# Windowed attention and mixture of experts: the product of P and V with 16 matmuls of 130 columns, and attention's pipeline one step longer

## The chip, the core and the metric

The kernel runs on one core of a Trainium2 chip. The core has five engines with queues of their own: TensorE (PE, its weight loads are shown as PEld), VectorE (DVE), ScalarE (ACT), GpSimd (POOL) and SyncE (SP), which here issues nearly all DMAs. The metric is the device time of one execution in microseconds (us).

## What is computed

Attention over 8 batches, 8 heads, 576 positions of 64 values. The first four heads see the last 32 positions, the other four see every fourth of the last 128. Its output, one row of 512 values for each of 4608 tokens, goes through a two-level choice of one expert out of 16 and that expert's two layers (512 to 1024 to 512).

```python
scores = scale * np.matmul(q, k.transpose(0, 1, 3, 2))
mask_plain = (rel >= 0) & (rel < window)                                   # heads 0 to 3
mask_dil = (rel >= 0) & (rel < window * dilation) & (rel % dilation == 0)  # heads 4 to 7
scores = scores - np.max(scores, axis=-1, keepdims=True)
attn = np.exp(scores)
attn = attn / (np.sum(attn, axis=-1, keepdims=True) + 1e-09)
out = np.matmul(attn, v)
...
for g in range(G):            # group by argmax of x @ w_group, expert by argmax of xg @ w_expert
    h = np.maximum(xg[mask_e] @ w1[g, e], 0.0)
    out[tok_idx] = combined[:, None] * (h @ w2[g, e])
```

## The kernel before

Attention runs as 36 tiles (`NT`), nine (`NJ`) for each of four pairs of batches. The dilated heads are laid out so that they are windows of 32 as well. A tile n holds 64 query positions of two batches and eight heads, in two halves a of 32 queries, and each half sees 64 keys. The main loop runs over steps s, and in one step several tiles are in work, each in another stage:

- `scores(s)`: a matmul with the identity puts the mask into PSUM (L263), then 16 float32 matmuls of 128 rows by 32 columns of weights (the queries) and 128 columns of keys are added (L275). DVE takes the row maxima (L285) and subtracts them (L286).
- `softexp(s)`: ACT takes the exponentials and writes p (L291).
- `transpose_p(s-1)`: PE turns p with four 128x128 transposes (L298), ACT copies the result to one of two buffers pt (L299).
- `av(s-2)`: 32 float32 matmuls (L308), each with 64 rows by 32 columns of weights (a piece of P turned) and 65 columns of V, which are 64 values and a column of constants that gives the softmax denominator. Half a = 1 reads V as loaded (`vt`), half a = 0 reads a copy shifted by 32 positions (`vs`), which POOL makes in `shift_v(s+2)` (L125, L131). ACT copies the denominators (L318).
- `normalise(s-2)`: DVE takes reciprocals (L334) and multiplies (L336) to x; `store(s-2)`: SP writes x to DRAM with two DMAs (L349).
- `transpose_x(s-3)`: four transposes (L360), which ACT copies to xT (L362, L364).

In between, `spend` runs pieces of the routing of a pair of batches whose nine tiles are complete (`route`, up to a budget of 1.8 in the units of a table of costs for each step): matmuls L377, L388, L447, L449, L524, and many small DVE operations. From the middle on, `run(wq)` loads one chunk of expert weights in a step (L630) and splits it into two float16 parts on ACT and DVE (L644, L641). At the last steps `run(eb[0], ...)` adds early pieces of the experts' layers. After the loop the experts follow one after the other: L759 (first layer), L818 (second), L740 (turning gathered rows).

The queues of PE, ACT, DVE and SP run in the order in which this code is written (`manual_schedule`); POOL's order is set by the tile framework's scheduler. In a step SP issues, in this order, the loads of q(s+4), k and v(s+3) and the two stores of x. Each waits for its buffer to be free, and each DMA on SP signals one of eight semaphores in turn, so that an issue also waits until the DMA eight issues earlier has landed.

A float32 matmul appears in the trace as two weight loads and two matmuls, a transpose or a 16-bit matmul as one of each.

Of the kernel before, what the change touches and what calls it, by code (L numbers as in the profile page):

```python
# [8 lines left out]
F32 = mybir.dt.float32  # L9
# [3 lines left out]
AF = mybir.ActivationFunctionType  # L13
ALU = mybir.AluOpType
# [3 lines left out]
P = 128  # L18
B, H, S, D = 8, 8, 576, 64
# [5 lines left out]
NJ = S // 64  # L25
NT = NBP * NJ
# [4 lines left out]
SCALE = 0.125  # L31
# [14 lines left out]
NWST2 = 3  # L46
BUDGET = 1.8
COST = (0.21, 0.3, 0.21, 0.62, 0.36)
NQ, NK, NV, NVS, NPT = 4, 6, 5, 4, 2
EARLY_STEPS = {NT - 1: 1, NT: 2, NT + 1: 2, NT + 2: 2}  # L50
TAIL = (
    "R0w0wr0rrrrrrrrrrr1rrrr0rr1r1rr1r1rr1rrB1w12w1ww112w2w2w2w2O2O2O2O2O2O"
# [12 lines left out]
def moe_attention_kernel(ctx, tc, q, k, v, cmask, wgate, wpack, out):  # L65
    nc = tc.nc
# [11 lines left out]
    id32 = cp.tile([P, P], F32, name="id32")  # L78
# [16 lines left out]
    att = ExitStack()  # L95
    apool = lambda name, bufs=1, **kw: att.enter_context(tc.tile_pool(name=name, bufs=bufs, **kw))
    psA = apool("psA", 1, space=PSUM)
    vp = apool("vp", NV)
    qp = apool("qp", NQ)
    kr = apool("kp").tile([P, 2, 2 * NK, 8, 32], F32, name="kr")  # L100
    pt = [apool(f"pt{i}").tile([P, 4, P], F32, name=f"pt{i}") for i in range(NPT)]
# [15 lines left out]

    def load_v(n):
        if n < NT:
            vt[n] = vp.tile([P, 8, 65], F32, name="vt")  # L120
            nc.sync.dma_start(vt[n], v[n])

    def shift_v(n):
        vs[n] = vp.tile([P, 8, 65], F32, name="vs", bufs=NVS)
        nc.gpsimd.tensor_scalar(vs[n], vt[n], 1.0, 1.0, ALU.mult, ALU.mult)  # L125
        for r in range(2):
            odd = slice(64 * r, 64 * r + 32)
            if n % NJ == 0:
                nc.gpsimd.memset(vs[n][odd], 0.0)
            else:  # L130
                nc.gpsimd.tensor_scalar(vs[n][odd], vt[n - 1][odd], 1.0, 1.0, ALU.mult, ALU.mult)  # L131

    nc.vector.memset(kr[:, :, 0 : NK + 1 : NK], 0.0)
    nc.sync.dma_start(masks[:, 0:2], cm[:, 0:2])
# [82 lines left out]
    ap = apool("ap", 3)  # L217
# [69 lines left out]
        dd[n] = d  # L287

    def softexp(n):
        p = ap.tile([P, 8, 64], F32, name="p", bufs=2)  # L290
        nc.scalar.activation(p, dd.pop(n), AF.Exp, scale=SCALE)  # L291
        st[n] = p

    def transpose_p(n):
        p = st.pop(n)
        t = psT.tile([P, 4, P], F32, name="t", tag="t")
        for c in range(4):
            nc.tensor.transpose(t[:, c, :], p[:, 2 * c : 2 * c + 2, :].rearrange("p a b -> p (a b)"), id32)  # L298
        nc.scalar.copy(pt[n % NPT], t)  # L299

    def av(n):
        o = psA.tile([P, 2, 512], F32, name="o", tag="o")
        for c in range(4):
            for w in range(2):
                for bb in range(2):
                    for a in range(2):
                        j = bb * 2 + a
                        nc.tensor.matmul(  # L308
                            o[32 * j : 32 * j + 32, w, c * 65 : c * 65 + 65],
                            pt[n % NPT][64 * w : 64 * w + 64, c, 32 * j : 32 * j + 32],  # L310
                            (vs, vt)[a][n][64 * w : 64 * w + 64, bb * 4 + c, :],
                            start=True,
                            stop=True,
                        )
        oo[n] = o
        den = ap.tile([P, 2, 4], F32, name="den")
        ov = o[:, :, 0:260].rearrange("p k (s c) -> p k s c", c=65)
        nc.scalar.activation(den, ov[:, :, :, 64], AF.Copy, bias=1e-9 / SX)  # L318
        dn[n] = den
# [10 lines left out]
    def normalise(n):  # L330
        o = oo.pop(n)
        ov = o[:, :, 0:260].rearrange("p k (s c) -> p k s c", c=65)
        den = dn.pop(n)
        nc.vector.reciprocal(den, den)  # L334
        x = ap.tile([P, 4, 2, 64], F32, name="x", bufs=5)
        nc.vector.tensor_tensor(  # L336
            x.rearrange("p s w c -> p w s c"),
            ov[:, :, :, 0:64],
            den.unsqueeze(3).broadcast_to([P, 2, 4, 64]),
            ALU.mult,  # L340
        )
        st[n] = x

    def store(n):
        x = st[n]
        bp, J = n // NJ, n % NJ
        for bb in range(2):
            row = (2 * bp + bb) * S + 64 * J
            nc.sync.dma_start(xd[row : row + 64], x[64 * bb : 64 * bb + 64].rearrange("p s w c -> p (s w c)"))  # L349
# [546 lines left out]
    man = ExitStack()  # L896
    ET = mybir.EngineType
    man.enter_context(tc.manual_schedule(engines={ET.PE, ET.Activation, ET.DVE, ET.SP}))
    for s in range(NT + 3):
        ripe = bool(gate)  # L900
        if s < NT:
            scores(s)
        if 0 <= s - 1 < NT:
            transpose_p(s - 1)
        if 0 <= s - 2 < NT:
            av(s - 2)
        if s < NT:
            softexp(s)
        if 0 <= s - 2 < NT:
            if ripe:  # L910
                gate.clear()
            normalise(s - 2)
        if start:
            n = start.pop()
            routes.append(route(n))
# [4 lines left out]
        load_q(s + 4)  # L920
        load_k(s + 4 - s % 2, s % 2)
        load_v(s + 3)
        if 0 <= s - 2 < NT:
            store(s - 2)
        if 0 <= s - 3 < NT:
            transpose_x(s - 3)
        flush()
        if s + 2 < NT:
            shift_v(s + 2)
# [13 lines left out]
        if eb:  # L943
            run(eb[0], EARLY_STEPS.get(s, 0))
        run(wq)
        if s >= 3 and (s - 3) % NJ == NJ - 1:
            bp = (s - 3) // NJ
            if bp < NBP - 1:
                start.append(bp)
        run(eq)  # L950
# [198 lines left out]
def layout(q, k, v, moe_w_group, moe_w_expert, moe_w1, moe_w2):  # L1149
# [13 lines left out]
    ka = np.stack([a.transpose(0, 4, 7, 5, 1, 2, 3, 6) for a in kg], axis=1).reshape(NT // 2, 2, 2, 64, 2, 256)  # L1163
    ka = ka.transpose(0, 2, 3, 4, 1, 5).reshape(NT // 2, 2, 64, 1024)
    vw = vs.reshape(NBP, 2, 2, 2, 2, 3, 3, 2, 32, D)[..., ::-1, :, :]
    va = vw.transpose(0, 5, 6, 4, 7, 8, 1, 2, 3, 9).reshape(NT, P, 8, D)
    va = np.concatenate([va, np.full_like(va[..., :1], 1.0 / SX)], axis=-1)

    cmask = np.full((2, 2, 32, len(MASKS), 2, 64), -1e9, np.float32)
# [45 lines left out]
```

## Time and profile before

| what | value |
|---|---|
| time, median of 3 runs | 597.36 us (597.07 to 603.14) |
| the profiled execution's own time | 598.75 us |
| its span in the trace | 597.0 us |
| PE busy in the span | 561.4 us (94%) |
| DVE, ACT, POOL busy | 389.5, 326.4, 241.9 us |
| mean granted share of TensorE's clock | 0.991 |

The attention loop fills the first 160 us or so of the span, the mixed end of attention and the routing of the last pair reaches to about 200 us, and the experts fill the rest. A busy share says how long an engine had an instruction in work. The end of a matmul is modelled, so matmuls that follow each other seem to overlap, and a busy PE may be a slowed one.

### The profile page before, as it was taken

How to read it: one execution, taken by the hardware profiler on the slowest of the kernel's cores; microseconds unless marked ns; L12 is line 12 of the kernel's file. 1: busy time of each engine (PE TensorE's matmuls, PEld its weight loads, DVE VectorE, ACT ScalarE, POOL GpSimd, SP SyncE). 2: the span in 40 equal slices, each digit the busy share in tenths (PEclk: the TensorE clock that was granted, in tenths of full speed). 3: DMA queues.
4: the chain of work that ended last, by engine and by line, in shares of the span. 5: the costliest groups of instructions: out<-in, count | busy, mean ns of one | idle time of the engine just before them, and what ended most of it. 6: DMA issues, size and time to landing. Idle time of an engine off the chain costs nothing.

```text
span 597.0 us, 18617 instructions
## 1 busy us (share of the span) xinstructions
PE 561.4 (94%) x7588; PEld 393.8 (66%) x7588; DVE 389.5 (65%) x804; ACT 326.4 (55%) x650; POOL 241.9 (41%) x313
## 2 busy tenths in 40 slices
PE   5888989889698999999999999999999999999995
PEld 3665767566485757765657566666767757767873
DVE  5664876988957833784778695565745766766720
ACT  2554665775555624774455546455655755656521
POOL 4644473636714605161415153442623503423411
PEclk9999999989999999999999999999999999999998
DMA  7998797898473227885677576756867578777300
GB/s 227 307 287 259 230 288 243 285 368 293 99 262 104 80 66 280 284 262 164 198 207 240 176 236 193 223 182 212 250 220 240 197 219 287 234 242 247 94 28 31
DMA packets 48313, 127.52 MB, mean 214 GB/s; under 512 B 7629, under 2 KB 8531, under 8 KB 48226
## 3 DMA queue, kind: packets, MB, share of 16 engines
q1 hardware_dynamic: 40466, 105.33, 55.8%
q0 software_dynamic: 7760, 20.99, 10.2%
q8 instruction: 61, 1.00, 0.7%
q14 instruction: 26, 0.21, 0.1%
HBM read 107.40 MB, written 19.22 MB: 212 GB/s over the span
## 4 chain that ended last, share of the span: by engine, by line
PE 67%; issue 3%; DVE 2%; ACT 1%; POOL 0%; POOLq 0%; ACTq 0%
PE y L818 32%; PE a L759 31%; PE pt L740 3%; DVE mv L505 1%; PE lt_ps L377 0%; PE tx L360 0%; PE o L308 0%; POOL out L779 0%; PE rp L685 0%; PE tb_ps L524 0%; DVE wb1l L641 0%; PE t L298 0%; ACT wb1h L644 0%; ACT room L766 0%; ACT off L243 0%
## 5 line engine op out<-in xcount | busy, mean ns | idle before, releaser
L709 POOL DMA_INDIRECT xr<-xd,sent x80 | 94.5, 1181 | 33.7 <-issue 21.8
L818 PEld LDWEIGHTS <-hh 128*128 128x128 f16 (+14 forms) x960 | 67.3, 99 | 57.6 <-issue 2.5
L779 POOL DMA_INDIRECT out<-yr,sent x30 | 31.0, 1032 | 179.2 <-ACT yr L792 152.7
L767 DVE SCALAR_TENSOR_TENSOR hl<-a,hh 128x256 f16<-128x256 f32 (+14 forms) x136 | 57.1, 422 | 64.1 <-ACT hh L766 64.0
L766 ACT ACTIVATE hh<-a 128x256 f16<-128x256 f32 (+14 forms) x136 | 51.7, 385 | 50.3 <-PE a L759 49.7
L759 PE MATMUL a<-xh,wb1h 128*128 128x256 f16 (+7 forms) x288 | 76.6, 270 | 0.0
L759 PE MATMUL a<-xh,wb1l 128*128 128x256 f16 (+7 forms) x288 | 76.5, 269 | 0.0
L759 PE MATMUL a<-xl,wb1h 128*128 128x256 f16 (+7 forms) x288 | 76.5, 269 | 0.0
L742 DVE TENSOR_TENSOR xl<-pt,xh 128x512 f16<-128x512 f32 (+14 forms) x42 | 24.6, 590 | 73.9 <-ACT xh L741 73.9
L759 PE MATMUL a<-xh,wa1h 128*128 128x186 f16 (+7 forms) x256 | 70.8, 277 | 0.0
L759 PE MATMUL a<-xl,wa1h 128*128 128x186 f16 (+7 forms) x256 | 70.7, 277 | 0.0
L759 PE MATMUL a<-xh,wa1l 128*128 128x186 f16 (+7 forms) x256 | 70.7, 277 | 0.0
L792 ACT ACTIVATE yr<-y,cs 128x512 f32<-128x512 f32 (+4 forms) x30 | 20.7, 688 | 88.7 <-PE y L818 59.5
L759 PEld LDWEIGHTS <-wa1h 128*128 128x128 f16 x640 | 59.0, 98 | 11.5 <-issue 0.3
L759 PEld LDWEIGHTS <-wb1h 128*128 128x128 f16 x576 | 54.3, 98 | 9.6 <-issue 0.2
L818 PE MATMUL y<-wb2h,hh 128*128 128x512 f16 (+7 forms) x272 | 59.7, 305 | 0.0
L818 PE MATMUL y<-wb2l,hh 128*128 128x512 f16 (+7 forms) x272 | 59.5, 304 | 0.0
L818 PE MATMUL y<-wb2h,hl 128*128 128x512 f16 (+7 forms) x272 | 59.5, 304 | 0.0
L818 PE MATMUL y<-wa2h,hh 128*128 128x512 f16 (+7 forms) x208 | 56.8, 331 | 0.0
L818 PE MATMUL y<-wa2h,hl 128*128 128x512 f16 (+7 forms) x208 | 56.6, 330 | 0.0
L818 PE MATMUL y<-wa2l,hh 128*128 128x512 f16 (+7 forms) x208 | 56.6, 330 | 0.0
L818 PEld LDWEIGHTS <-hl 128*128 128x128 f16 (+14 forms) x480 | 34.4, 99 | 25.1
(190 smaller groups left out, 1227.8 us busy)
## 6 DMA issues: line engine op xcount, KB each, us to landing
w<-wpack SPq DMA_DIRECT2D x128, 512.0 KB, 4.8
vt<-v SPq DMA_DIRECT2D x36, 260.0 KB, 4.7
qb<-q SPq DMA_DIRECT2D x36, 256.0 KB, 4.7
xd<-x SPq DMA_DIRECT2D x72, 128.0 KB, 4.2
kr<-k SPq DMA_DIRECT2D x34, 256.0 KB, 5.1
xr<-xd,sent POOLq DMA_INDIRECT x80, 4.5
kr<-k SPq DMA_DIRECT2D x4, 128.0 KB, 3.0
out<-yr,sent POOLq DMA_INDIRECT x30, 3.8
```

Source lines behind the costliest of these rows:

```text
L505: nc.vector.scalar_tensor_tensor(mv[:, t], high.rearrange("p e k -> p (e k)").unsqueeze(1).broadcast_to([P, 4, NE * NK4]), hl[:, 1, t0 + t ...
L709: nc.gpsimd.indirect_dma_start(out=xr[:, 256 * h : 256 * h + 256], out_offset=None, in_=xd[0:known].rearrange("n (h c) -> (n h) c", h=2), ...
L740: nc.tensor.transpose(pt[:, c, 0:n], xr[0:n, c * P : c * P + P], id32[0:n, 0:n])
L742: nc.vector.tensor_tensor(xl[:, :, t * P : t * P + n], pt[:, :, 0:n], xh[:, :, t * P : t * P + n], ALU.subtract)
L759: nc.tensor.matmul(a[:, 0:cap], ww[:, c * FF + f * P : c * FF + f * P + P], xx[:, c, 0:cap], start=(i == 0), stop=(i == len(mm) - 1),)
L766: nc.scalar.activation(hh[:, f, 0:cap], a[:, 0:cap], AF.Relu)
L767: nc.vector.scalar_tensor_tensor(hl[:, f, 0:cap], a[:, 0:cap], 0.0, hh[:, f, 0:cap], ALU.max, ALU.subtract)
L779: ins = nc.gpsimd.indirect_dma_start(out=out.rearrange("n (g c) -> (n g) c", g=g), out_offset=bass.IndirectOffsetOnAxis(ap=at, axis=0), in ...
L792: nc.scalar.activation(yr[0:n, :], yp[0:n, :], AF.Copy, scale=cs[0:n, t : t + 1])
L818: nc.tensor.matmul(yp[P // g * j : P // g * j + n, 0 : DM // g], h[:, f, t * P : t * P + n], ww[:, f * DM + DM // g * j : f * DM + DM // g ...
```

## The change

V is no longer multiplied in two halves of 64 rows. The V tile gets two column blocks, one for the rows of each of the two windows w (plain and dilated), and the rows of the other window in a block are zero: `[P, 2, 520]` instead of `[P, 8, 65]`. The rows of the two windows alternate over the partitions. One matmul then takes all 128 rows and gives both windows at once, so `av` issues 16 matmuls of 128 rows by 32 columns of weights and 130 columns. To fit, `softexp` writes p with the two windows interleaved.

The V tiles become a ring of six (`NV`) that is never reallocated: each is set to zero once by ACT when it is first used, and each load writes only the non-zero half of each block, with two DMAs of 64 rows. The shifted copies become a ring of five (`NVS`); POOL makes one with two operations on 64 partitions by 1040 elements, before it was one on 128 by 520 and two on 32 by 520. Since the rows alternate, `normalise` writes x through another view of the same tile.

The pipeline gets one more step: `av`, `normalise` and `store` work on tile s-3 instead of s-2, `transpose_x` on s-4, and the loop has 40 iterations instead of 39. `transpose_p(s-1)` moves from behind `scores(s)` to the end of the step's work on PE and ACT, behind `transpose_x`. The routing of a pair starts one step later.

```diff
--- before.py
+++ after.py
@@ -46,7 +46,7 @@
 NWST2 = 3
 BUDGET = 1.8
 COST = (0.21, 0.3, 0.21, 0.62, 0.36)
-NQ, NK, NV, NVS, NPT = 4, 6, 5, 4, 2
+NQ, NK, NV, NVS, NPT = 4, 6, 6, 5, 2
 EARLY_STEPS = {NT - 1: 1, NT: 2, NT + 1: 2, NT + 2: 2}
 TAIL = (
     "R0w0wr0rrrrrrrrrrr1rrrr0rr1r1rr1r1rr1rrB1w12w1ww112w2w2w2w2O2O2O2O2O2O"
@@ -95,7 +95,7 @@
     att = ExitStack()
     apool = lambda name, bufs=1, **kw: att.enter_context(tc.tile_pool(name=name, bufs=bufs, **kw))
     psA = apool("psA", 1, space=PSUM)
-    vp = apool("vp", NV)
+    vp = [[apool(f"v{k}{i}").tile([P, 2, 520], F32, name=f"v{k}{i}") for i in range(n)] for k, n in enumerate((NV, NVS))]
     qp = apool("qp", NQ)
     kr = apool("kp").tile([P, 2, 2 * NK, 8, 32], F32, name="kr")
     pt = [apool(f"pt{i}").tile([P, 4, P], F32, name=f"pt{i}") for i in range(NPT)]
@@ -117,18 +117,22 @@
 
     def load_v(n):
         if n < NT:
-            vt[n] = vp.tile([P, 8, 65], F32, name="vt")
-            nc.sync.dma_start(vt[n], v[n])
+            vt[n] = vp[0][n % NV]
+            if n < NV:
+                nc.scalar.activation(
+                    vt[n].rearrange("p w n -> p (w n)"), id32[:, 0:1].broadcast_to([P, 1040]), AF.Copy, scale=0.0
+                )
+            for w in range(2):
+                nc.sync.dma_start(vt[n][w:P:2, w], v[n, w:P:2].rearrange("p s c -> p (s c)"))
 
     def shift_v(n):
-        vs[n] = vp.tile([P, 8, 65], F32, name="vs", bufs=NVS)
-        nc.gpsimd.tensor_scalar(vs[n], vt[n], 1.0, 1.0, ALU.mult, ALU.mult)
-        for r in range(2):
-            odd = slice(64 * r, 64 * r + 32)
-            if n % NJ == 0:
-                nc.gpsimd.memset(vs[n][odd], 0.0)
-            else:
-                nc.gpsimd.tensor_scalar(vs[n][odd], vt[n - 1][odd], 1.0, 1.0, ALU.mult, ALU.mult)
+        vs[n] = vp[1][n % NVS]
+        odd, even = slice(0, 64), slice(64, P)
+        nc.gpsimd.tensor_scalar(vs[n][even], vt[n][even], 1.0, 1.0, ALU.mult, ALU.mult)
+        if n % NJ == 0:
+            nc.gpsimd.memset(vs[n][odd], 0.0)
+        else:
+            nc.gpsimd.tensor_scalar(vs[n][odd], vt[n - 1][odd], 1.0, 1.0, ALU.mult, ALU.mult)
 
     nc.vector.memset(kr[:, :, 0 : NK + 1 : NK], 0.0)
     nc.sync.dma_start(masks[:, 0:2], cm[:, 0:2])
@@ -287,31 +291,32 @@
         dd[n] = d
 
     def softexp(n):
-        p = ap.tile([P, 8, 64], F32, name="p", bufs=2)
-        nc.scalar.activation(p, dd.pop(n), AF.Exp, scale=SCALE)
+        p = ap.tile([P, 4, 64, 2], F32, name="p", bufs=2)
+        d = dd.pop(n).rearrange("p (c w) k -> p c w k", w=2)
+        nc.scalar.activation(p.rearrange("p c k w -> p c w k"), d, AF.Exp, scale=SCALE)
         st[n] = p
 
     def transpose_p(n):
         p = st.pop(n)
         t = psT.tile([P, 4, P], F32, name="t", tag="t")
         for c in range(4):
-            nc.tensor.transpose(t[:, c, :], p[:, 2 * c : 2 * c + 2, :].rearrange("p a b -> p (a b)"), id32)
+            nc.tensor.transpose(t[:, c, :], p[:, c].rearrange("p k w -> p (k w)"), id32)
         nc.scalar.copy(pt[n % NPT], t)
 
     def av(n):
         o = psA.tile([P, 2, 512], F32, name="o", tag="o")
         for c in range(4):
-            for w in range(2):
-                for bb in range(2):
-                    for a in range(2):
-                        j = bb * 2 + a
-                        nc.tensor.matmul(
-                            o[32 * j : 32 * j + 32, w, c * 65 : c * 65 + 65],
-                            pt[n % NPT][64 * w : 64 * w + 64, c, 32 * j : 32 * j + 32],
-                            (vs, vt)[a][n][64 * w : 64 * w + 64, bb * 4 + c, :],
-                            start=True,
-                            stop=True,
-                        )
+            for bb in range(2):
+                for a in range(2):
+                    j = bb * 2 + a
+                    vv = (vs, vt)[a][n].rearrange("p w (s c) -> p w s c", c=65)
+                    nc.tensor.matmul(
+                        o[32 * j : 32 * j + 32, c // 2, c % 2 * 130 : c % 2 * 130 + 130],
+                        pt[n % NPT][:, c, 32 * j : 32 * j + 32],
+                        vv[:, :, bb * 4 + c],
+                        start=True,
+                        stop=True,
+                    )
         oo[n] = o
         den = ap.tile([P, 2, 4], F32, name="den")
         ov = o[:, :, 0:260].rearrange("p k (s c) -> p k s c", c=65)
@@ -334,7 +339,7 @@
         nc.vector.reciprocal(den, den)
         x = ap.tile([P, 4, 2, 64], F32, name="x", bufs=5)
         nc.vector.tensor_tensor(
-            x.rearrange("p s w c -> p w s c"),
+            x.rearrange("p (k s) w c -> p k (s w) c", k=2),
             ov[:, :, :, 0:64],
             den.unsqueeze(3).broadcast_to([P, 2, 4, 64]),
             ALU.mult,
@@ -896,20 +901,18 @@
     man = ExitStack()
     ET = mybir.EngineType
     man.enter_context(tc.manual_schedule(engines={ET.PE, ET.Activation, ET.DVE, ET.SP}))
-    for s in range(NT + 3):
+    for s in range(NT + 4):
         ripe = bool(gate)
         if s < NT:
             scores(s)
-        if 0 <= s - 1 < NT:
-            transpose_p(s - 1)
-        if 0 <= s - 2 < NT:
-            av(s - 2)
+        if 0 <= s - 3 < NT:
+            av(s - 3)
         if s < NT:
             softexp(s)
-        if 0 <= s - 2 < NT:
+        if 0 <= s - 3 < NT:
             if ripe:
                 gate.clear()
-            normalise(s - 2)
+            normalise(s - 3)
         if start:
             n = start.pop()
             routes.append(route(n))
@@ -920,10 +923,12 @@
         load_q(s + 4)
         load_k(s + 4 - s % 2, s % 2)
         load_v(s + 3)
-        if 0 <= s - 2 < NT:
-            store(s - 2)
         if 0 <= s - 3 < NT:
-            transpose_x(s - 3)
+            store(s - 3)
+        if 0 <= s - 4 < NT:
+            transpose_x(s - 4)
+        if 0 <= s - 1 < NT:
+            transpose_p(s - 1)
         flush()
         if s + 2 < NT:
             shift_v(s + 2)
@@ -943,8 +948,8 @@
         if eb:
             run(eb[0], EARLY_STEPS.get(s, 0))
         run(wq)
-        if s >= 3 and (s - 3) % NJ == NJ - 1:
-            bp = (s - 3) // NJ
+        if s >= 4 and (s - 4) % NJ == NJ - 1:
+            bp = (s - 4) // NJ
             if bp < NBP - 1:
                 start.append(bp)
         run(eq)
@@ -1163,7 +1168,7 @@
     ka = np.stack([a.transpose(0, 4, 7, 5, 1, 2, 3, 6) for a in kg], axis=1).reshape(NT // 2, 2, 2, 64, 2, 256)
     ka = ka.transpose(0, 2, 3, 4, 1, 5).reshape(NT // 2, 2, 64, 1024)
     vw = vs.reshape(NBP, 2, 2, 2, 2, 3, 3, 2, 32, D)[..., ::-1, :, :]
-    va = vw.transpose(0, 5, 6, 4, 7, 8, 1, 2, 3, 9).reshape(NT, P, 8, D)
+    va = vw.transpose(0, 5, 6, 7, 8, 4, 1, 2, 3, 9).reshape(NT, P, 8, D)
     va = np.concatenate([va, np.full_like(va[..., :1], 1.0 / SX)], axis=-1)
 
     cmask = np.full((2, 2, 32, len(MASKS), 2, 64), -1e9, np.float32)
```

PE's queue, from the end of one step's product of P and V to the start of the next, before (t is P turned, tx is x turned, o the product, s the scores):

```order
L308 MATMUL o<-vt,pt_122 32x65
L360 MATMUL tx<-id_73,x 128x128 x4
L263 LDWEIGHTS idb
L263 MATMUL s<-masks,idb 128x512
L275 MATMUL s<-kr,qb 32x128 x16
L298 MATMUL t<-id_73,p 128x128 x4
L308 MATMUL o<-vs,pt_118 32x65
L308 MATMUL o<-vt,pt_118 32x65
```

The same place after the change:

```order
L313 MATMUL o<-v_120,pt_163 32x130
L365 MATMUL tx<-id_73,x 128x128 x4
L303 MATMUL t<-id_73,p 128x128 x4
L267 LDWEIGHTS idb
L267 MATMUL s<-masks,idb 128x512
L279 MATMUL s<-kr,qb 32x128 x16
L313 MATMUL o<-v_148,pt_159 32x130
L313 MATMUL o<-v_124,pt_159 32x130
```

The four transposes of P (t) stand behind those of x now, and the product follows the scores directly; a step has 16 rows of L313 where it had 32 of L308.

SP's queue for one step before, with what each issue waits for (DMAHW0 to DMAHW7 are the semaphores of the DMAs eight issues earlier; the others are engines):

```order
L107 DMA qb<-q 128x512 [waits DMAHW0_49,PE_49]
L116 DMA kr<-k 64x2x512 [waits DMAHW1_49]
L121 DMA vt<-v 128x520 [waits DMAHW2_49,PE_49,Pool_49]
L349 DMA xd<-x 64x512 [waits DMAHW3_49,DVE_49]
L349 DMA xd<-x 64x512 [waits DMAHW4_49]
```

And after the change:

```order
L107 DMA qb<-q 128x512 [waits DMAHW5_49,PE_49]
L116 DMA kr<-k 64x2x512 [waits DMAHW6_49]
L126 DMA v_112<-v 64x520 [waits DMAHW7_49,PE_49,Pool_49]
L126 DMA v_112<-v 64x520 [waits DMAHW0_49]
L354 DMA xd<-x 64x512 [waits DMAHW1_49,DVE_49]
L354 DMA xd<-x 64x512 [waits DMAHW2_49]
```

A step has six issues instead of five, and the eight semaphores come round in one step and a third instead of one and three fifths.

## Rows read from the trace of the kernel before

**Rows 1.** Page, DMA queues: packets, MB, share of 16 engines.
```profile
q8 instruction: 61, 1.00, 0.7%
```

**Rows 2.** Stretches: us, busy (x count) by engine, granted clock, DMA share, GB/s.
```profile
16.80:52.50 35.70, 30.40 (x954) 22.19 (x946) 21.84 (x64) 18.57 (x48) 19.57 (x33) 1.00 0.91 289
52.50:100.40 47.90, 44.71 (x1261) 33.14 (x1260) 33.42 (x69) 29.14 (x75) 25.70 (x46) 1.00 0.82 251
100.40:158.30 57.90, 49.36 (x1372) 35.81 (x1369) 51.19 (x111) 38.31 (x90) 34.18 (x56) 0.97 0.82 271
158.30:200.00 41.70, 35.74 (x549) 27.55 (x550) 30.34 (x87) 27.23 (x72) 18.37 (x28) 0.96 0.52 162
200.00:577.00 377.00, 377.00 (x3154) 257.58 (x3153) 240.46 (x456) 205.42 (x351) 132.77 (x118) 1.00 0.65 207
```

**Rows 3.** PE in time, one step: start us, us, engine, line, operation.
```profile
66.78 0.38 PE L263 MATMUL s<-masks,idb 128*128 128x512 bf16 x1
67.09 1.08 PE L275 MATMUL s<-kr,qb 128*32 128x128 f32 x32
68.10 0.66 PE L298 MATMUL t<-id,p 128*128 128x128 f32 x4
68.69 0.24 PE L308 MATMUL o<-vs,pt 64*32 64x65 f32 x1
...
69.48 0.66 PE L360 MATMUL tx<-id,x 128*128 128x128 f32 x4
69.97 0.38 PE L263 MATMUL s<-masks,idb 128*128 128x512 bf16 x1
```

**Rows 4.** PE in time, inside one product of P and V.
```profile
118.15 0.22 PE L308 MATMUL o<-vt,pt 64*32 64x65 f32 x1
119.79 0.24 PE L308 MATMUL o<-vs,pt 64*32 64x65 f32 x1 [1.43 <-issue]
```

**Rows 5.** Stretches between two such waits' ends (columns as rows 2).
```profile
47.36:51.79 4.43, 3.59 (x127) 2.65 (x127) 2.28 (x4) 2.11 (x5) 1.86 (x3) 1.00 0.88 299
114.67:119.79 5.12, 3.69 (x127) 2.75 (x127) 5.00 (x9) 5.01 (x12) 4.76 (x8) 1.00 1.01 361
```

**Rows 6.** Waits, 0 to 170 us: who waited for whom, total us, times, longest.
```profile
PE o L308 <- issue: 9.3, 10, 1.7
PE t L298 <- ACT p L291: 7.3, 6, 2.6
PE s L275 <- issue: 2.3, 3, 1.9
```

**Rows 7.** SP in time, issues that follow each other.
```profile
31.39 0.54 SPq L107 DMA_DIRECT2D qb<-q  x1
31.97 0.59 SPq L116 DMA_DIRECT2D kr<-k  x1
32.67 0.54 SPq L121 DMA_DIRECT2D vt<-v  x1
33.30 1.09 SPq L349 DMA_DIRECT2D xd<-x  x2
34.44 0.48 SPq L209 DMA_DIRECT2D xd<-xe  x1
```

**Rows 8.** DMA issues, 20 to 55 us: KB each, median us to landing.
```profile
vt<-v SPq DMA_DIRECT2D x9, 260.0 KB, 4.9
xd<-x SPq DMA_DIRECT2D x18, 128.0 KB, 4.2
```

**Rows 9.** The same, 105 to 150 us.
```profile
vt<-v SPq DMA_DIRECT2D x9, 260.0 KB, 5.6
```

**Rows 10.** Groups of instructions, 0 to 160 us: busy us, mean ns of one.
```profile
L131 POOL TENSOR_SCALAR vs<-vt 32x520 f32<-32x520 f32 x63 | 40.6, 644 | 8.3 <-DMA xe<-xd,ente 3.4
L364 ACT COPY xT<-tx 128x256 f32<-128x256 f32 x21 | 13.7, 652 | 0.0
L362 ACT COPY xT<-tx 128x256 f32<-128x256 f32 x32 | 11.6, 363 | 4.0 <-PE tx L360 4.0
```

## The prediction

> **What bounds the kernel now.** I read the stretches by stage first, to find where time can come from at all. From 200 to 577 us PE is busy for 377.00 of 377.00 us: the experts are bound by PE, and whatever starts them earlier ends the kernel earlier by as much. Before that there are four stages [rows 2]: A (16.8 to 52.5, nine steps without routing), B (to 100.4, eleven steps with two routings), C (to 158.3, twelve and a half steps with routing and expert weights), D (to 200, the end of attention). PE is idle for 5.3, 3.2, 8.5 and 6.0 us in them, 23.0 in all. In C another engine is nearly full: DVE is busy for 51.19 of 57.90.
>
> Then one step of PE in time [rows 3]. Undisturbed, it takes 69.97 - 66.78 = 3.19 us: mask 0.31, scores 1.01, P turned 0.59, the product 0.79, x turned 0.49. Stage A has 35.7 / 9 = 3.97 a step, so 0.78 a step is lost where DVE is busy for 61% and ACT for 52% of the time. The waits say where: "issue" before a product of P and V for 9.3 us and before scores for 2.3, and PE waits 7.3 us for the exponentials that it is to turn [rows 6]. The first kind comes in the middle of a product, 32 matmuls that need nothing new: 1.43 us of idle after a run of records a few ns apart [rows 4]. Between the ends of two such waits lie 127 matmuls and 127 weight loads, in 4.43 us in A and 5.12 in C [rows 5]; with two semaphore instructions that makes 256. And the queue "instruction" brought 1.00 MB in 61 packets, 16.4 KB each, which over 256 instructions is 64 bytes for one [rows 1]. So I read these waits as PE running out of code: a block of 256 takes 4.4 to 5.1 us to come, while the step's 210 instructions (mask 2, scores 64, P 8, product 128, x 8) would be done in 3.19 us. At 210 in each step the code alone asks for 3.6 to 4.2 us, and A has 3.97.
>
> The Trainium skill says otherwise (Runtime: NRT & Kernel Launch, Instruction fetch mechanics): code comes in 16 KiB blocks of 256 instructions, which fits the packets, but the fetch is "hidden" by the pace of issue. By the page the idle time would have another cause and would stay; by the rows it repeats with the block. I go by the rows, and keep the other as a rival below.
>
> **The product.** It falls from 32 to 16 matmuls, from 128 to 64 instructions, so a step has 146. At 4.4 to 5.1 us for 256, the code asks for 2.5 to 2.9 us a step, less than PE's own work: these waits should go almost wholly. What it costs: the new product has the form of the scores, 128 rows by 32 columns of weights, and 130 columns instead of 128. The scores take 1.01 from start to next start, so I take 1.01 x 130 / 128 = 1.03 instead of 0.79, 0.24 more. The transposes of P then follow those of x, a full array after a full array; x to mask takes 0.49, P to product 0.59, so 0.10 comes back. Step: 0.31 + 1.01 + 1.03 + 0.49 + 0.49 = 3.33, that is 0.14 more, 5.0 us over 36 steps (8.6 if nothing comes back). Fewer, larger matmuls are no gain by themselves here.
>
> **P turned last, one step more.** PE no longer turns p(s-1) just after scores(s), where it waited 7.3 us in all; p is a whole step old when its turn comes, and its copy on ACT is needed only two steps later. This gives back between 0 and 7.3. Behind that turn now stand the routing matmuls of the step, but nobody waits for it soon. What PE can wait for next is the single PSUM buffer o: the product needs x(s-4) written by DVE in the step before, and it comes 0.59 earlier in the step. Where DVE is late (C), this wait takes over. The 40th iteration holds only the last transposes of x; total PE work is the same, and the early expert pieces of the iterations before lie ahead of it. Routing starts one step later, so 1.8 us of DVE's budget moves from before the last scores to after them.
>
> **V's loads.** Two DMAs instead of one. Five issues of SP that follow each other take 34.44 - 31.39 = 3.05 us, 0.61 each [rows 7], so six take 3.66: more than PE's 3.33. SP runs up to four steps ahead with q and three with k and v, so it may fall behind for a while, but A is nine steps long. In a step with a weight load there are seven. Each issue also waits for the DMA eight earlier: at 3.66 a step that is 8/6 x 3.66 = 4.9 us before. Landings in A take 4.2 (half-size stores) to 4.9 (whole V) [rows 8], so this just holds. Behind a late V load stand the stores of x and the next q and k.
>
> **Hidden work.** POOL's copies were three of 0.644 [rows 10]; two of twice the length cost between 0.644 and 1.29 each, so 1.3 to 2.6 us a step against 1.9, and they are needed a step later than before. The exponentials are written at a stride of 8 bytes. The nearest row is the copy with a stride of 16, 652 ns for 256 elements against 363 at none, so 512 cost 0 to 0.58 more; in C that is at most 7.2 on 38.3 busy of 57.9. Six zero fills on ACT of 1040 elements, each at most 1.5 (363 x 1040 / 256), lie in the first steps, where PE and ACT wait for the first data. All three I take as 0. If ACT's slack in C went, the 7.2 would come onto the path.
>
> **The sum, by stage.** A: PE's floor 9 x 3.33 = 30.0, SP's 9 x 3.66 = 32.9, against 35.7: a gain of 2.8 to 5.7; I take 3.5, nearer to SP. B: 3.2 of idle less 11 x 0.14 = 1.5, so -1.5 to 1.7; I take 1.0, since the two long routings hold no wait of these. C: DVE's 51.2 leaves 6.7, from which the short gaps between 111 operations do not go; 0 to 6.7, I take 2.5. The half clock of part of C (0.97 on the mean) may go with the waits; it is in these 2.5. D: the longest wait for p, 2.6, lies here; 0 to 2.6, I take 1.0, since DVE's lateness was its cause. Together 8.0. The profiled execution took 598.75 us, so 590.75; the median of the runs is 1.39 below it, so **589.4**.
>
> **Rivals**, all on the median's scale, where 1% (6.0 us, about what can be told from no change) lies at 591.4 and 603.3.
> - The forecast, a gain of 5 to 12 (585.4 to 592.4): 0.50.
> - All idle time goes: 23.0 less 5.0 of longer products, a gain of 18, 579.4. For it: p and the loads have slack everywhere. Against it: DVE in C. A gain of 12 to 19: 0.14.
> - The next bound takes nearly all: SP's six issues or DVE hold the step where it was, a gain of 0 to 5, 595: 0.20.
> - Landings decide, slower. The eight semaphores allow one step in 6/8 of a landing, so A is slower from a landing of 8/6 x 3.97 = 5.3 us on. At the 5.6 that V shows from 105 to 150 us [rows 9] a step takes 4.2 in A (9 x 0.23 = 2.1 lost), and with seven issues 4.9 in C against 4.63 (12.5 x 0.27 = 3.4 lost); with 1.5 in B that is 7.0: 604.4. Against it: eight DMAs in flight hold fewer bytes when V comes in halves. 0.08.
> - The waits are not for code and stay (the page's rule above); only the longer products count, 5.0 more: 602.4. Against it: 254 records between them, twice in rows far apart. 0.08.
>
> The forecast's part below 591.4 is 6/7 of 0.50, 0.43; with 0.14 that is 0.57 faster. Slower is most of the fourth and the upper end of the fifth, 0.07. The rest, 0.36, is the same. From 579 to 599 leaves out the last two, and little else.
>
> **What would show it.** Right: 36 x 64 = 2,304 fewer PE instructions and so nine fewer code packets; no idle marked "issue" inside L313; a step of 3.3 to 3.7 in A; products that take 1.03 to the next start. SP's six issues without a gap in A would show that it has become the bound, and PE then waits for q or k. In C, DVE nearly without waits. Wrong: waits inside products as before, or PE waiting for POOL's copies or for x(s-4).

## The result, and the profile after

The changed kernel takes 606.69 us (median of 20 runs, 604.12 to 610.16); in the same rounds the kernel before takes 601.75. The ratio of the means is 1.0092, with a 95% interval of 1.0068 to 1.0117: a little slower, where 589.4 and a gain were forecast. Chips differ by some per cent, so every run below is given as a ratio to the kernel before on its own chip.

What the change was to remove is gone. The queue that brings code shows nine packets fewer than in [rows 1] (columns: packets, MB, share of 16 engines):

```profile
q8 instruction: 52, 0.85, 0.6%
```

PE in time (start, duration, engine, line, operation, in brackets the idle time before it and what ended it) shows the new step, and then what stops it:

```profile
36.98 0.38 PE L267 MATMUL s<-masks,idb 128*128 128x512 bf16 x1
37.29 1.08 PE L279 MATMUL s<-kr,qb 128*32 128x128 f32 x32
38.19 1.07 PE L313 MATMUL o<-v,pt 128*32 128x130 f32 x32
39.19 0.65 PE L365 MATMUL tx<-id,x 128*128 128x128 f32 x4
39.68 0.60 PE L303 MATMUL t<-id,p 128*128 128x128 f32 x4
40.12 0.38 PE L267 MATMUL s<-masks,idb 128*128 128x512 bf16 x1
43.20 1.08 PE L279 MATMUL s<-kr,qb 128*32 128x128 f32 x32 [2.71 <-DMA kr<-k]
```

From mask to mask an undisturbed step takes 40.12 - 36.98 = 3.14 us, 0.05 less than in [rows 3], and no product stops inside any more. But then PE stands for 2.7 us in front of the scores until K lands. The waits from 0 to 170 us (engine, line and releaser: us in total, times, longest) name it:

```profile
PE s L279 <- DMA kr<-k: 17.8, 8, 4.2
PEld s L279 <- DMA kr<-k: 16.5, 11, 4.5
PE o L313 <- DVE val L483: 4.4, 2, 3.9
```

In the kernel before, K cost PE 3.0 us in this stretch. The third line holds one stop of 3.9 us behind the last scores, where PE waits for DVE and not for K. SP in time, about two of its rounds, shows why K is late:

```profile
38.26 0.61 SPq L116 DMA_DIRECT2D kr<-k  x1
38.97 1.17 SPq L126 DMA_DIRECT2D v<-v  x2
40.24 1.62 SPq L354 DMA_DIRECT2D xd<-x  x2
41.96 0.54 SPq L107 DMA_DIRECT2D qb<-q  x1
42.54 0.59 SPq L116 DMA_DIRECT2D kr<-k  x1
43.24 1.18 SPq L126 DMA_DIRECT2D v<-v  x2
44.52 1.18 SPq L354 DMA_DIRECT2D xd<-x  x2
45.79 0.54 SPq L107 DMA_DIRECT2D qb<-q  x1
```

SP issues one load or store behind the other, with gaps of some 0.1 us, and waits for nothing: 45.79 - 41.96 = 3.83 us for a round of six issues, against PE's 3.14. The load of K at 38.26 belongs to SP's round 7 and serves the scores of step 10. PE began its own step 7 at 30.7, so this load was issued 7.5 us behind it; K landed at 43.16, 4.9 us after its issue, and the scores began at 43.20. I measure the distance at the issue that opens a round and call it **SP's lag**: from the mask of step s on PE to the issue of q(s+4) on SP, 7.1 us in this round. In the kernel before it stays between 1.5 and 6.6 us for steps 5 to 31, 3.3 in the mean (the smallest value is that of an SP that waits for PE). In the changed kernel it is 4.3 to 14.2, 9.2 in the mean.

By stage, in the same bounds as [rows 2] (us; busy time and instructions of PE, PEld, DVE, ACT, POOL; granted clock, DMA share, GB/s):

```profile
16.80:52.50 35.70, 29.17 (x651) 24.50 (x652) 22.23 (x60) 17.97 (x48) 23.10 (x24) 0.95 0.87 262
52.50:100.40 47.90, 43.47 (x853) 35.30 (x854) 32.40 (x66) 28.28 (x74) 27.73 (x35) 0.93 0.82 241
100.40:158.30 57.90, 46.07 (x950) 37.73 (x942) 49.14 (x100) 36.01 (x86) 33.34 (x43) 0.97 0.90 292
```

PE is idle for 6.5, 4.4 and 11.8 us where it had been for 5.3, 3.2 and 8.5, and its granted clock is below full in all three stages: it fell to the lower level (1.2 of 2.4 GHz) at about 20.7, 68.5, 123 and 167.5 us, each time in or right behind a stop of 3.3 to 4.5 us (the first three for K, the last for DVE), and stayed there for 3.4 to 6.8 us. In the kernel before this happened twice up to 200 us, for 3.4 us each. The mask of step 12 starts earlier than before (49.17 against 52.53), that of step 35 later (158.3 against 155.7), and the matmuls of the last routing (L452, before L447) at 189.4 against 183.5. So the changed kernel is 3.4 us ahead at the end of A, 0.8 at the end of B, 2.5 behind at the end of C and 5.9 at the last routing. Behind it the traces run nearly alike: the spans differ by 603.1 - 597.0 = 6.1.

### The profile page after: what moved, and what is told of

The parts are those of the page before. It is cut to its first block, busy times and chain, and to the rows that moved or that the text cites. A ratio compares the mean times of both kernels' runs of the same rounds, so it can differ in the third digit from the quotient of the medians.

```text
span 603.1 us, 16369 instructions
## 1 busy us (share of the span) xinstructions
PE 559.8 (93%) x6436; PEld 403.4 (67%) x6436; DVE 394.7 (65%) x804; ACT 330.4 (55%) x656; POOL 251.4 (42%) x277
## 4 chain that ended last, share of the span: by engine, by line
PE 67%; issue 2%; DVE 1%; ACT 1%; POOL 0%; POOLq 0%; ACTq 0%
PE y L823 31%; PE a L764 30%; PE pt L745 3%; PE o L313 1%; PE lt_ps L382 0%; PE tx L365 0%; PE tb_ps L529 0%; POOL out L784 0%; PE rp L690 0%; DVE mv L510 0%; ACT off L247 0%; DVE wb1l L646 0%; ACT ohl L248 0%; ACT wb1h L649 0%; ACT room L771 0%
## 5 line engine op out<-in xcount | busy, mean ns | idle before, releaser
L279 PE MATMUL s<-kr,qb 128*32 128x128 f32 x1152 | 42.4, 292 | 19.1 <-DMA kr<-k 17.8
L131 POOL TENSOR_SCALAR v<-v 64x1040 f32<-64x1040 f32 x36 | 40.4, 1121 | 40.4 <-DMA v<-v 34.6
```

The costliest lines, as they stand in the source:

```text
L131: nc.gpsimd.tensor_scalar(vs[n][even], vt[n][even], 1.0, 1.0, ALU.mult, ALU.mult)
L279: nc.tensor.matmul(s[32 * j : 32 * j + 32, c].rearrange("p w k -> p (w k)"), qv[:, (sl * 2 + a) * 32 : (sl * 2 + a) * 32 + 32], kr[:, :, k ...
```

## Experiments

**Theory 1**: SP's time in issues, six a step, lets SP fall behind PE until K is late. **Rival A**: the DMA engines, or loads of 64 rows as such, are what is slow. **Rival B**: the new order of the steps costs it. A fourth possibility, that SP waits for semaphores of DMAs that have not landed, is looked up in the traces below. In the code cuts, "..." stands for lines left out.

### First four: one part undone, or one part alone

`one_store`, on the changed kernel:

```diff
-        for bb in range(2):
-            row = (2 * bp + bb) * S + 64 * J
-            nc.sync.dma_start(xd[row : row + 64], x[64 * bb : 64 * bb + 64].rearrange("p s w c -> p (s w c)"))
+        rows2 = xd[2 * bp * S : (2 * bp + 2) * S].rearrange("(b r) c -> b r c", b=2)[:, 64 * J : 64 * J + 64]
+        nc.sync.dma_start(rows2, x.rearrange("p s w c -> p (s w c)"))
```

> The changed kernel, but each step's result x is stored by one DMA of 128 rows in place of two of 64, so that SP issues five DMAs a step and not six; bytes, products and the order of the work stay. Theory 1 (SP's issues bound attention: six at 0.64 us are 3.83 us a round, and PE's own step is 3.13 us): SP's round falls to 3.2 us, the stops of PE for K (3 to 4.5 us each, seven of them up to 170 us) mostly go, with them the half-clock stretches behind them, and the time is 596 to 601 us. Rival A (the transfers themselves are late: 64-row loads of V, DMA share 0.87): same bytes, same waits for K, 605 to 608 us. Rival B (the longer pipeline or P's new place in the step): 605 to 608 us.

Measured: 1.1325 (1.1291 to 1.1358). The edit took an issue away and broke something else. SP in time:

```profile
68.69 0.55 SPq L353 DMA_DIRECT2D xd<-x  x1
69.33 3.90 SPq L107 DMA_DIRECT2D qb<-q  x1
73.29 1.59 SPq L116 DMA_DIRECT2D kr<-k  x1
```

The store landed 12.8 us after its issue (the last update of its semaphore is at 81.47). From 70.0 to 73.0 us the packets of the trace show 2.1 of 16 DMA engines at work with 51 GB/s: the transfer of 2 by 64 rows was spread over the two of its outer dimension. The Trainium skill (DMA: Bandwidth & Descriptors, Why a DMA increments its semaphore by 16 and not by 1) says so: the number of engines follows from the slowest dimension of the transfer, and the trace agrees with its 2.1. And the issue behind it held SP for 3.90 us instead of 0.54. So this run says nothing about theory 1, but it shows that an issue can be held while an earlier transfer is not yet taken off.

`v_act`, on the changed kernel:

```diff
-                nc.sync.dma_start(vt[n][w:P:2, w], v[n, w:P:2].rearrange("p s c -> p (s c)"))
+                (nc.sync, nc.scalar)[w].dma_start(vt[n][w:P:2, w], v[n, w:P:2].rearrange("p s c -> p (s c)"))
```

> The changed kernel, but the second of V's two DMAs of a step is issued by ScalarE's queue; SP keeps five issues a step, the stores stay two. Theory 1 (SP's issues): the K waits go, and ScalarE pays one issue a step, some 0.6 us of its idle third; 597 to 603 us. Rival A (the transfers): the K waits stay, 605 to 608 us. Rival B (the order): 605 to 608 us. If this one gains and the single store does not, the stores' own split is not what costs.

Measured: 1.0108 (1.0076 to 1.0141), so no gain, against theory 1 as I had put it. SP had five issues, but its lag was 9.5 us in the mean. Its own waits (16 to 150 us) say why:

```profile
SPq L354 <- DMA v<-v: 16.9, 12, 2.9
SPq L107 <- DMA v<-v: 3.2, 3, 1.9
```

In the trace both queues' loads use the same eight semaphores. ACT issues its half of V when its own work lets it, and SP then waits for that load to land before it may use the semaphore again. All its waits for V add up to 25.4 us. The issues saved came back as waits.

`before_split`, on the kernel before:

```diff
-            nc.sync.dma_start(vt[n], v[n])
+            for w in range(2):
+                nc.sync.dma_start(vt[n][64 * w : 64 * w + 64], v[n, 64 * w : 64 * w + 64])
```

> The kernel before, but V is loaded by two DMAs of 64 rows each, so that SP issues six DMAs a step; nothing else differs. Theory 1 (SP's issues): SP's round becomes 3.8 us against a PE step of 3.19 us and the code stops, K waits appear in the kernel before as well, and it is slower by 2 to 6 us: 604 to 608 us. Rival A (the transfers): slower too, but with V or K landings longer by 1 us or more at a spacing of the issues that is not longer. Rival B (the order of the steps): no change, 601 to 603 us.

Measured: 1.0191 (1.0145 to 1.0237). The kernel before with nothing changed but V's load in two has the K waits of the changed one, 16.5 us on PE and 16.1 on PEld, and a lag of 10.0 us:

```profile
PE s L276 <- DMA kr<-k: 16.5, 8, 4.8
```

`order_only`, on the kernel before (rings of V one longer too):

```diff
...
-        if 0 <= s - 1 < NT:
-            transpose_p(s - 1)
-        if 0 <= s - 2 < NT:
-            av(s - 2)
+        if 0 <= s - 3 < NT:
+            av(s - 3)
...
+        if 0 <= s - 1 < NT:
+            transpose_p(s - 1)
...
```

> The kernel before with the changed order alone: attention's pipeline one step longer, P transposed last in a step, rings of V one longer; products, V's loads and the exponential as before. Theory 1 (SP's issues): SP keeps five issues, no K waits appear, PE's stops for code inside the products stay; 600 to 603 us, less by 1 to 2 us if P's wait was worth something, more by 2 to 3 us if the extra step at the end of attention is what it costs. Rival B (the order is what costs): 605 to 608 us.

Measured: 1.0012 (0.9985 to 1.0040). The order as a whole (P's wait gone, one more step at the end) neither costs nor gives anything that can be measured, and the lag is 3.5 us. Rival B has fallen as the cause of the loss.

### Issues without transfers, and transfers with fewer issues

`before_tiny`, on the kernel before: `nc.sync.dma_start(tiny[0:1], cmask[0:1, 0:32])` behind each load of V.

> The kernel before with one more DMA a step on SP, of 64 bytes into a tile that nothing reads: one issue more, no transfer worth the name. Theory 1 (SP's count of issues bounds attention once it is six a step): K waits appear as in the changed kernel, and it is slower by 0.7 to 1.9% of the kernel before's time on the same chip (4 to 11 us; V's loads split in two cost 1.9%). Rival A (the DMA engines, or V's loads of 64 rows as such): nothing is transferred, so no K waits and a ratio of 0.998 to 1.003.

Measured: 1.0027 (0.9990 to 1.0063), less than I expected. This issue holds SP for 0.25 us in the median, where one of 64 or 128 rows takes 0.53 to 0.59. A round without long issues then takes about 3.5 us, and the lag is 6.5: K waits of 12 us in all on PE and PEld, and a loss too small to be told.

`x_pair`, on the changed kernel: x of two steps in one tile, stored every second step (the ninth tile of a pair alone):

```diff
...
+        if J % 2 == 0 and J < NJ - 1:
+            return
+        m = 1 + J % 2
         for bb in range(2):
-            row = (2 * bp + bb) * S + 64 * J
-            nc.sync.dma_start(xd[row : row + 64], x[64 * bb : 64 * bb + 64].rearrange("p s w c -> p (s w c)"))
+            row = (2 * bp + bb) * S + 64 * (J + 1 - m)
+            nc.sync.dma_start(
+                xd[row : row + 64 * m].rearrange("(m i) c -> i m c", m=m),
+                x[64 * bb : 64 * bb + 64, 0:m].rearrange("p m s w c -> p m (s w c)"),
+            )
...
```

> The changed kernel with x stored for two steps at a time: two DMAs of 64 rows by 4 KB every second step in place of two of 64 rows by 2 KB every step, so five issues a step in the mean; bytes and the rest stay. (Its outer dimension stays 64 rows, since the single store of 2 by 64 rows went to two DMA engines.) Theory 1 (SP): SP's round falls to 3.2 us in the mean, the K waits fall from 34 us to under 12, ratio to the kernel before 0.990 to 1.001. Rival A (the DMA engines are full: share 0.82 to 0.90, same bytes): K waits stay, ratio 1.005 to 1.012. Rival B (the order of the steps): ratio 1.005 to 1.012.

Measured: 0.9942 (0.9908 to 0.9976), 1.5% below the changed kernel, with the same bytes. The K waits of the changed kernel shrink to one line, and both of its waits lie in the first 20.2 us:

```profile
PE s L279 <- DMA kr<-k: 6.1, 2, 3.8
```

and in the first two stages the DMA engines carry more, not less, than in the changed kernel:

```profile
16.80:52.50 35.70, 29.83 (x649) 25.03 (x650) 22.23 (x60) 17.48 (x45) 24.11 (x24) 0.93 0.90 275
52.50:100.40 47.90, 44.74 (x902) 36.92 (x901) 36.00 (x67) 28.64 (x74) 28.63 (x36) 0.95 0.87 266
```

So the DMA engines were not what held the changed kernel up. Lag: 4.4 us. SP's own time in a round, its issues and the gaps of less than 0.15 us between them, shows the bound in the mean of rounds 9 to 19. In the changed kernel it is 4.39 us, the whole round, and SP never waits longer than such a gap. With the paired store it is 3.74 of a round of 3.86; in the kernel before 3.36 of 4.17.

`before_x_pair`, the same edit on the kernel before:

> The kernel before with the same paired store, so four issues a step in the mean. Theory 1 (SP): in the kernel before SP is only now and then late (K waits of some us), so a gain of 0 to 1%, ratio 0.990 to 1.000, less than the same edit brings the changed kernel. Rival A: no change, ratio 0.998 to 1.003.

Measured: 1.0003 (0.9969 to 1.0036), lag 2.7. With five issues SP does not bound the kernel before, and saving one of the five brings it nothing.

`x_pair_tiny2`, on `x_pair`: behind each half of V a DMA of 64 bytes that nothing reads.

> The changed kernel with the paired store (0.994 of the kernel before), and two more DMAs of 64 bytes a step on SP that nothing reads. One such issue took 0.25 us of SP in the median, so that two with their gaps are 0.6 us, as much as one issue of 64 rows: SP's round is that of the changed kernel again, and no transfer is added. Theory 1 (SP's time in issues makes K late): the K waits come back and with them most of the loss, ratio 1.002 to 1.010. Rival A (the number or form of the transfers): it stays at 0.991 to 0.998.

Measured: 1.0220 (1.0185 to 1.0256), above my range: 2.8% for two issues that move nothing. They take 0.43 us each here, not 0.25; SP in time:

```profile
51.01 0.59 SPq L108 DMA_DIRECT2D qb<-q  x1
51.63 0.94 SPq L117 DMA_DIRECT2D kr<-k  x1
52.69 0.57 SPq L127 DMA_DIRECT2D v<-v  x1
53.30 0.43 SPq L128 DMA_DIRECT2D tiny<-cmask  x1
53.78 0.48 SPq L127 DMA_DIRECT2D v<-v  x1
54.31 0.43 SPq L128 DMA_DIRECT2D tiny<-cmask  x1
54.84 0.36 SPq L108 DMA_DIRECT2D qb<-q  x1
```

This round has no store and still takes 3.83 us; the lag is 10.3, and the K waits are back (with 8.5 us for q on PEld):

```profile
PE s L281 <- DMA kr<-k: 15.7, 8, 3.3
```

SP's own time in rounds 9 to 19 is 4.36 us again, as in the changed kernel. The two issues also bring the eight semaphores round sooner, but SP's waits for DMAs that have not landed add up to 2.8 us from 16 to 150 us, so that is not it. This is the run that shows theory 1: SP's time in issues, without any bytes worth the name, makes K late. It loses more than the changed kernel; SP's own time is longer in rounds 20 to 30 (4.65 against 4.27), but that this is the reason is not shown.

`split_pair`, on `before_split`: the paired store.

> The kernel before with V loaded by two DMAs of 64 rows (alone 1.019) and the paired store (alone 1.000): five issues a step in the mean, as in the kernel before. Theory 1 (SP's time in issues): nearly all of the 1.9% goes, ratio 0.997 to 1.006. Rival A (loads of 64 rows are slow as such): it stays, ratio 1.010 to 1.020.

Measured: 1.0064 (1.0031 to 1.0096): two thirds of the 1.9% go, and the lag falls from 10.0 to 4.1 us. The last 0.6% lies just above the range that theory 1 had named; whether loads of 64 rows cost that by themselves stays open.

### What else there is to gain

`short_pipe`, the changed kernel in the order of the kernel before (the reverse of `order_only`):

> The changed kernel with the order of the kernel before: attention's pipeline as long as there, P transposed right behind the next scores; 16 products of 130 columns, V's two loads and the exponential as in the changed kernel. Theory 1 (SP): PE's waits for P come back (some us of 7 in 0 to 170 us), but PE is bound by K anyway and the extra step at the end of attention (3 us) is saved: ratio 1.002 to 1.010, K waits as in the changed kernel. Rival B (the order is what costs): the loss goes, ratio 0.985 to 1.000.

Measured: 1.0131 (1.0075 to 1.0187), not better than the changed kernel's 1.0092, lag 9.3. So the order costs nothing there either.

`x_q_pair`, on `x_pair`: q for two steps in one DMA, every odd step.

```diff
...
-            qb[n] = qp.tile([P, 512], F32, name="qb")
-            nc.sync.dma_start(qb[n], q[n])
+            two = qp.tile([P, 2, 512], F32, name="qb", bufs=NQ // 2)
+            nc.sync.dma_start(two, q[n : n + 2].rearrange("n p c -> p n c"))
+            qb[n], qb[n + 1] = two[:, 0], two[:, 1]
...
```

> The changed kernel with the paired store and Q loaded for two steps at a time as well (one DMA of 128 rows by 4 KB every odd step), 4.5 issues a step in the mean. If SP still bounds with five issues: 0.984 to 0.992. If with five issues the bound is already PE's own step and the work of DVE at the end of attention: 0.991 to 0.998, and the K waits no smaller in sum than with the paired store alone.

Measured: 0.9941 (0.9915 to 0.9967), the same as with the paired store alone. At five issues SP is no longer the bound.

`x_pair_late`, on `x_pair`: `EARLY_STEPS = {NT: 1, NT + 1: 2, NT + 2: 2, NT + 3: 2}`.

> The changed kernel with the paired store, and the pieces of the first expert pass that are put into attention's last steps moved one step later, as the pipeline is one step longer. If these pieces stand ahead of the products in the last steps and hold them up (PE's wait of 3.9 us at 163.7 us in the changed kernel): gain of 1 to 4 us against the paired store alone, 0.988 to 0.993. If they only fill waits for DVE that are there anyway: 0.993 to 1.000.

Measured: 1.0009 (0.9979 to 1.0040), worse than `x_pair` and above both ranges. That the early pieces hold the last products up finds no support here. What they lose by coming later was not followed up.

The last three ran on one chip: `short_x_pair` (the paired store and the old order), the changed kernel, and `x_pair` again.

> The changed kernel with the paired store and the order of the kernel before (attention's pipeline as long as there, P transposed right behind the next scores). If the extra step at the end is what is left of the loss: the stretch from the last scores to the last routing matmuls is 3 us shorter than with the longer pipeline, PE's waits for P cost 1 to 4 us of it again, and the ratio is 0.986 to 0.994. If the longer pipeline is worth its price once SP is not in the way, as it was with six issues (1.009 against 1.013): 0.996 to 1.004.

> The changed kernel as it is, beside the paired store on the same chip: ratio 1.006 to 1.013, K waits of some 34 us in 0 to 170 us.

> The changed kernel with the paired store, as before: ratio 0.990 to 0.998, K waits under 12 us. Its last scores come 4 to 8 us earlier than in the changed kernel on this chip, and the end of attention moves by as much, the stretch behind the last scores being the same.

Measured: 0.9984 (0.9955 to 1.0013), 1.0066 (1.0034 to 1.0099) and 0.9914 (0.9884 to 0.9945), in this order. From the three traces (start of a mask on PE and of the last routing matmuls, in us; lag in the mean of steps 5 to 31):

| kernel | lag | step 12 | step 23 | step 35 | last routing | end of PE |
|---|---|---|---|---|---|---|
| changed | 9.2 | 50.9 | 101.9 | 161.3 | 195.0 | 607.5 |
| paired store | 4.4 | 46.9 | 98.2 | 150.3 | 184.2 | 600.0 |
| paired store, old order | 5.2 | 49.5 | 99.8 | 154.6 | 186.1 | 600.3 |

The paired store brings the last scores 11.0 us forward, more than the 4 to 8 expected, and the last routing by 10.8; the stretch between them is the same, 33.7 and 33.9. Of this, 7.5 remain at the end. K waits fall from 12.7 us on PE and 12.6 on PEld (25.3 in all, where 34 were expected) to 8.6 and 0.9. With the old order the stretch behind the last scores is 31.5, shorter by the step that was saved, but the scores come 4.3 us later. The longer pipeline is worth its price once SP is out of the way, and the changed kernel with the paired store is faster than the kernel before, by 0.6 and 0.9% in two runs.

## Why the prediction was wrong

- **Code for PE, and the step: right.** The waits inside products went, with nine packets, and the step is 3.14 us. Two more readings bear it out. In the kernel before, PE has eleven idle times marked "issue" of more than 0.3 us from 5 to 170 us, and each ends 1.3 to 1.6 us after a packet of 16 KB on the queue that brings code has ended. And stops inside a product (over 0.3 us, up to 170 us) are there 9 times in the kernel before and 12 times in `order_only`, but never in the changed kernel nor in `short_pipe`: the number of matmuls decides, not their order. The product's price was over-estimated: the step was to grow by 0.14 and shrank by 0.05. In time, the product takes 1.00 from its start to the next (39.19 - 38.19), about the 1.03 named; what was missed is the scores before it, now 0.90 from start to start (38.19 - 37.29) instead of 1.01, and P's turn before the mask, 0.44.
- **V's loads: this is the step that failed.** The prediction says that SP's six issues take 3.66 us, more than PE's step, and that SP "may fall behind for a while, but A is nine steps long". The term was too small: six issues take 3.83 us where none is held, and in rounds 9 to 19 SP's own time is 4.39 us a round, since some issues are held (from 40 to 67 us five issues were longer by 0.45 to 1.1 us). That is more than the whole round of the kernel before there, 4.17. The lead was counted from the program (three and four steps), not from the trace: SP's lag could have been read there, and beside a step of PE without routing each round adds at least 0.69 us to it (3.83 - 3.14), so that nine steps cost 6.2 us, more than the 4.5 us that three steps of 3.14 leave beside K's landing of 4.9 (38.26 to 43.16). And the sum used SP's floor in stage A alone, and let B and C go without it, where the lag grows to 14 us. A came out as forecast, 3.4 us ahead at its end where 3.5 was taken; B lost 2.6 us and C 3.3, where gains of 1.0 and 2.5 had been taken.
- **The rival that ended slower had the right sign with the wrong mechanism.** It named landings and the eight semaphores. Landings became shorter (4.1 us in the median for half of V, where [rows 8] have 4.9 and [rows 9] 5.6 for the whole), and between 16 and 150 us SP waited for DMAs to land for 4.0 us in all. The third rival, that SP's six issues take the gain, was the right one in kind; it stopped at no change, because it let SP hold PE's step at 3.66 us, and SP's own time is longer than that.
- **P's wait: it went, and its worth is not shown.** It is gone in the changed kernel and in `order_only`, but `order_only` gives 1.0012, and in that run the extra step at the end counts as well; no run has the one without the other.
- **D: wrong sign.** 1.0 was to be gained. The stretch from the mask of step 35 to the last routing grew from 27.8 (155.7 to 183.5) to 31.1 us (158.3 to 189.4); the three traces on one chip put 2.4 of such a growth to the extra step (33.9 against 31.5). SP has no part in it, since the stretch is the same with six issues and with five (33.7 and 33.9). With the paired store, what the step gives earlier in attention pays for it.
- **POOL's copies, the exponentials, the zero fills, taken as 0:** measured 1.12 and 1.08 us for POOL's two, 683 ns for an exponential against 629 before, and 1.05 for a zero fill, all within the bounds named. No run separates them.
- **The size, without SP.** With the paired store the change gains 0.6 and 0.9% in two runs, 3.5 and 5.2 us of 601.75, where 8.0 were forecast: the rest of the sum is right in direction, and 1.5 to 2.3 times too large. The Trainium skill's rule against it (Runtime: NRT & Kernel Launch, Instruction fetch mechanics), that the fetch is hidden, does not agree with the traces: the stops of the kernel before end 1.3 to 1.6 us after a code packet, and with half of the product's instructions and nine packets fewer they are gone.

## What to carry over

Before a change that adds a DMA to each step of a loop, read in the trace how far the issuing queue runs behind the engine it feeds, and what one round of issues takes with its long ones; if the round is longer than the step that is left, the lead shrinks with every step. A faster engine makes that worse, since it is the difference of the two paces that eats the lead. That more buffers would only put the end of it off is argued; no run had them. Issues can be saved without touching a byte, by moving two steps' data in one DMA, as long as its outer dimension stays large (64 rows did no harm here, 2 cost 13%).

## What the runs showed of the hardware

- A DMA issue held SP for 0.53 to 0.59 us in the median for 64 and for 128 rows alike in the two kernels (0.37 for q in `x_pair_tiny2`), for 0.25 to 0.43 for a single row: half-size DMAs cost SP twice. Two issues of 64 bytes a step cost the whole kernel 2.8%. The Trainium skill (DMA: Bandwidth & Descriptors, Rules for kernel authors) advises one transfer over 128 partitions instead of two halves, since both run on the same engines; the runs agree with the advice (1.019 for two halves), but here most of it went into the issuing queue, since with the paired store two thirds came back.
- Long issues come with other transfers. In the changed kernel five issues from 40 to 67 us took 0.45 to 1.1 us longer than usual, and at each of the five moments a code packet of 16 KB was on its way, which takes 0.9 to 1.7 us as one packet. All twelve issues up to 110 us that are over 0.25 us longer than the median of their kind have such a packet beside them. For example this pair of stores, 2.26 us instead of 1.18, with a packet from 61.29 to 62.85:

```profile
61.61 2.26 SPq L354 DMA_DIRECT2D xd<-x  x2
```

  With `one_store` an issue behind a slow transfer took 3.90 us. That the code packet is the cause is argued from the coincidence, not shown by a run.
- A store whose outer dimension is 2 ran on two DMA engines, at 51 GB/s, and cost the kernel 13%.
- In the changed kernel PE's granted clock fell to 1.2 GHz at four of its stops of 3.3 to 4.5 us. The stop shown at 40.2 us (2.7 us between records, 3.1 from mask to scores) had none behind it. What a stop costs is thus more than its own length in some cases, and SP's pace does not tell in which. The lower clock is not what sets the changed kernel apart from the paired store: up to 200 us it holds for 17.1 us in the changed kernel and for 20.5 in `x_pair`, which is 1.5% faster.
